# Two fp32 mixture-of-experts stages behind an attention: where w_out's parts, the weight sums and the routing are made

## The chip, the core and the metric

The kernel runs on one core of a Trainium2 chip. The core has five engines with instruction queues of their own: TensorE (PE; matmuls, whose weight loads are listed apart as PEld), VectorE (DVE), ScalarE (ACT), GpSimd (POOL) and SyncE (SP), which here only issues DMA transfers. The metric is the device time of one execution in microseconds; runs are given by their median.

## The reference

Three stages, each on the output of the one before, all in fp32:

```python
# 1. linear attention with decay, 4 x 8 heads, 768 steps, head size 64
state = gamma * state + k_t (outer) v_t;   y_t = scale * q_t @ state
# 2. x is 3072 x 512; w_a, w_b are 512 x 1536, w_out is 1536 x 512
x = ((x @ w_a) * (x @ w_b)) @ w_out
# 3. eight experts, one per token: w1 is 512 x 1024, w2 is 1024 x 512
e = argmax(x @ w_gate)
out = softmax(x @ w_gate)[e] * sigmoid(x @ w_output_gate)[e] * (relu(x @ w1[e]) @ w2[e])
```

## The kernel before

**Precision.** An fp32 operand is split into a high and a low part (a rounded copy and the difference), and `mm3` (L107 to L110) makes one product of three matmuls: high by high, high by low, low by high. "Parts" below always means this pair.

**Token groups.** The second stage runs over 3072 tokens in four groups. Tokens 0 to 511 and 512 to 1023 are the direct groups j = 0 and j = 1: for each of 12 tiles f of 128 hidden units `proj` makes both projections, `gate` their product with its split (`gs`, L576 and L579), and `down` adds the tile before to four token tiles. Tokens 1024 to 2047 and 2048 to 3071 are j = 2 and j = 3. For these `block_of_sums` (L706) makes each hidden tile for 1024 tokens from seven products of quarter matrices (quarters of x and of the weights, their sums and differences: B11, B21, B22 and U1 to U4; the weight side of a tile lies in two *units*, loaded from the DRAM tensor `q_d` by `load_unit`), 6 matmuls of 512 columns each on the two banks p0 and p1. The results are combined on VectorE (a1 at L721, g2 at L735, b2 at L738, a1 at L746), GpSimd multiplies one half (L739) and VectorE the other, which is split (`gs`, L748 and L749). `down` adds the first 512 tokens at once; the second 512 wait in `later` for `later_pass` (L760), which splits them tile by tile (`later_split`, L754 to L757) and makes their down product.

**w_out.** `wo_d` in DRAM holds w_out in fp32. For each tile of each pass after the first (j = 1, both blocks, both later passes; 60 in all) `load_wo` (L537) loads 256 KB two tiles ahead and `split_wo` makes the parts, the high one on ScalarE (L545), the low one by a subtraction on GpSimd (L546; two on VectorE).

**Weight sums.** During j = 1 `sum_steps` loads for each of 12 tiles 512 KB, makes four sums and differences on GpSimd (L626), splits them on ScalarE and VectorE (L630, L631), and stores 1 MB to `q_d`. `x_steps` makes the sums and splits of x's quarters for a block (L660, L666), three of them on GpSimd.

**Attention** runs beside the second stage, in 12 chunks of 256 steps (4 to 7 in j = 1, 8 to 11 in the first block), in batches: decay products `qd` (L149) and `vd` (L158) on VectorE, or on GpSimd for the chunks in `Q_POOL` and `V_POOL`, then scores and outputs on TensorE.

**Routing.** Each of 24 tiles of 128 tokens gets its expert and its place in the table `tab_d`. On TensorE (`on_pe`) that is a transpose (L301), the logits (L310) and a rank matmul (L340). On VectorE (`on_dve`) a tile is loaded again (`x2r`, L359), eight dot products with the gate's columns `wcol` follow (`s_d`, L365), then the argmax (`s_m`, L370), upon which GpSimd gathers for each token the column of its expert's output gate (`wx`, an indirect transfer, L374), then the dot product with it (`s_o`, L396 to L402), and the rank (`s_r`, L344 to L349). Tiles 2 to 7 are routed so in the first block, 8 to 15 in the second, 0 and 1 on TensorE in j = 1.

**What sets the order.** Each engine works in program order, and the order is written out by hand: `slot()` is called at fixed places (3 in each tile of a direct group, 7 in each tile of a block, 1 in a later pass), and `spread` deals lists of steps over a range of slots. An instruction that waits holds up everything behind it on its engine; a DMA that waits on SyncE holds up the queue.

```python
def mm3(outp, wh, wl, rh, rl, start, stop, more=False):
    pe.matmul(outp, lhsT=wh, rhs=rh, start=start, stop=False, skip_group_check=more)
    pe.matmul(outp, lhsT=wh, rhs=rl, start=False, stop=False, skip_group_check=more)
    pe.matmul(outp, lhsT=wl, rhs=rh, start=False, stop=stop, skip_group_check=more)
```

## Time and profile before

| | us |
|---|---|
| three runs | 1086.79, 1082.97, 1084.02 (median 1084.02) |
| the profiled execution | 1076.0 |
| its span, first to last instruction | 1074.3 |
| TensorE busy | 995.1 (93%), 7314 matmuls |
| VectorE, ScalarE, GpSimd busy | 633.0, 398.7, 318.2 |
| mean granted clock of TensorE | 0.977 |

The stretches of the program, by TensorE's instructions in the trace: the start to 27 us, j = 0 to 142, j = 1 to 292, the first block to 470, its later pass to 515, the second block to about 680, its later pass to 741, then the experts to the end. A row of the profile that names a wait gives what the engine waited for; where it stands in the program follows from the tile's name and the line.

### The profile page before, as it was taken

Reading aid. Unit: us, or ns where it says so; the run is one execution under the profiler, and the core shown is the slowest. Engines: PE = TensorE matmul, PEld = TensorE weight load, DVE = VectorE, ACT = ScalarE, POOL = GpSimd, SP = SyncE. Lnnn points to the kernel's source line nnn. Section 1 sums busy time; section 2 is a strip of 40 time slices with the busy share of each in tenths; the row PEclk is TensorE's granted clock in tenths of the full one; section 3 lists DMA queues with packets and bytes.
Section 4 is the critical chain, followed back from the end, with each engine's and each line's share of the span. In section 5 each row is a group of like instructions: output and inputs, shape, how many; then the busy total and the mean of one; then the engine's idle time right before and its main releaser. Section 6 shows DMA issues by size and latency. Waiting matters only on the chain. (4 is left out here: it accounts for less than half of the span.)

```text
span 1074.3 us, 19807 instructions
## 1 busy us (share of the span) xinstructions
PE 995.1 (93%) x7314; PEld 802.6 (75%) x7315; DVE 633.0 (59%) x1383; ACT 398.7 (37%) x768; POOL 318.2 (30%) x282
## 2 busy tenths in 40 slices
PE   6899999869899999989899999788699999999997
PEld 5688887757667777767677777567589988889886
DVE  5899955644846666648466666466255553445541
ACT  3676742323422222235222222245154443344431
POOL 3211014856511222237232323242222220203211
PEclk8999999989899999999899999899999999999999
DMA  6999965989786564533655654333166553536620
GB/s 245 341 327 300 297 207 196 303 325 372 261 310 225 191 227 161 161 117 88 226 173 191 170 206 133 130 129 105 23 196 195 186 160 116 169 97 194 204 87 28
DMA packets 72776, 208.70 MB, mean 194 GB/s; under 512 B 12717, under 2 KB 22189, under 8 KB 67888
## 3 DMA queue, kind: packets, MB, share of 16 engines
q1 hardware_dynamic: 65520, 187.95, 53.5%
q0 software_dynamic: 6544, 18.41, 5.0%
q8 instruction: 82, 1.34, 0.5%
q10 hardware_dynamic: 576, 0.56, 0.1%
q14 instruction: 54, 0.44, 0.1%
HBM read 162.79 MB, written 45.01 MB: 193 GB/s over the span
## 5 line engine op out<-in xcount | busy, mean ns | idle before, releaser
L546 POOL TENSOR_TENSOR wos<-wo,wos 128x512 fp32r<-128x512 f32 x58 | 84.2, 1452 | 95.1 <-ACT wos L545 39.6
L888 DVE TENSOR_TENSOR ew<-wraw,ew 128x512 fp32r<-128x512 f32 x112 | 77.1, 690 | 55.0 <-ACT ew L887 54.5
L108 PE MATMUL ph<-xe,ew 128*128 128x384 f32 (+4 forms) x288 | 98.2, 341 | 1.8 <-DVE x L599 1.1
L854 DVE SCALAR_TENSOR_TENSOR hs<-ph,hs 128x384 fp32r<-128x384 f32 (+4 forms) x72 | 39.1, 543 | 97.0 <-ACT hs L853 97.0
L109 PE MATMUL ph<-xe,ew 128*128 128x384 f32 (+4 forms) x288 | 95.2, 331 | 0.3 <-DVE xe L839 0.3
L110 PE MATMUL ph<-xe,ew 128*128 128x384 f32 (+4 forms) x288 | 95.3, 331 | 0.0
L874 POOL DMA_INDIRECT out<-y,idx x27 | 27.2, 1006 | 228.3 <-ACT y L873 214.6
L887 ACT CAST ew<-wraw 128x512 fp32r<-128x512 f32 x112 | 68.9, 616 | 55.7 <-PE acc L110 51.6
L108 PE MATMUL p<-U,unit 128*128 128x512 f32 x192 | 77.8, 405 | 10.1 <-DVE b L738 8.3
L108 PE MATMUL acc<-ew,hs 128*128 128x512 f32 (+1 forms) x216 | 85.7, 397 | 1.2 <-DVE hs L854 1.2
L108 PE MATMUL acc<-wos,gs 128*128 128x512 f32 x192 | 81.3, 424 | 4.7 <-ACT gs L576 3.8
L109 PE MATMUL acc<-ew,hs 128*128 128x512 f32 (+1 forms) x216 | 85.4, 396 | 0.0
L110 PE MATMUL acc<-ew,hs 128*128 128x512 f32 (+1 forms) x216 | 85.0, 394 | 0.0
L108 PE MATMUL p<-xs,ar 128*128 128x512 f32 x192 | 78.7, 410 | 5.2 <-DVE g_sb L571 2.8
L365 DVE SCALAR_TENSOR_TENSOR junkd<-x2r,wcol 128x512 bf16<-128x512 f32 x112 | 76.7, 685 | 10.3 <-DMA x2r<-x_d 9.4
L110 PE MATMUL acc<-wos,gs 128*128 128x512 f32 x192 | 78.5, 409 | 2.3 <-DVE gs L749 1.6
L853 ACT ACTIVATE hs<-ph 128x384 fp32r<-128x384 f32 (+4 forms) x72 | 34.5, 479 | 118.7 <-PE ph L110 112.4
L109 PE MATMUL acc<-wos,gs 128*128 128x512 f32 x192 | 77.1, 402 | 0.0
L110 PE MATMUL p<-xs,ar 128*128 128x512 f32 x192 | 75.8, 395 | 0.3
L110 PE MATMUL p<-U,unit 128*128 128x512 f32 x192 | 75.7, 394 | 0.0
L109 PE MATMUL p<-xs,ar 128*128 128x512 f32 x192 | 75.5, 393 | 0.0
L109 PE MATMUL p<-U,unit 128*128 128x512 f32 x192 | 75.5, 393 | 0.0
(207 smaller groups left out, 2308.0 us busy)
## 6 DMA issues: line engine op xcount, KB each, us to landing
wraw<-in_ex SPq DMA_DIRECT2D x64, 512.0 KB, 3.9
unit<-q_d SPq DMA_DIRECT2D x24, 1024.0 KB, 5.5
unit<-q_d SPq DMA_DIRECT2D x24, 768.0 KB, 4.5
wo<-wo_d SPq DMA_DIRECT2D x60, 256.0 KB, 3.9
wide<-in_w_ab SPq DMA_DIRECT2D x24, 512.0 KB, 6.0
q_d<-qsum SPq DMA_DIRECT2D x12, 1024.0 KB, 7.5
qk<-in_qk SPq DMA_DIRECT2D x23, 512.0 KB, 6.6
vk<-in_vk SPq DMA_DIRECT2D x23, 512.0 KB, 7.4
```

Of the source, the lines that this page charges most:

```text
L108: pe.matmul(outp, lhsT=wh, rhs=rh, start=start, stop=False, skip_group_check=more)
L109: pe.matmul(outp, lhsT=wh, rhs=rl, start=False, stop=False, skip_group_check=more)
L110: pe.matmul(outp, lhsT=wl, rhs=rh, start=False, stop=stop, skip_group_check=more)
L365: dve.scalar_tensor_tensor(junk, st["x2"], 1.0, wcol[e], op0=ALU.mult, op1=ALU.mult, accum_out=st["lg"][:, e : e + 1])
L546: (eng or pool).tensor_tensor(w[:, 1], t, f32(w[:, 0]), op=ALU.subtract)
L853: act.activation(h[:, 0, :n], p[:, :n], AF.Relu)
L854: dve.scalar_tensor_tensor(h[:, 1, :n], p[:, :n], 0.0, f32(h[:, 0, :n]), op0=ALU.max, op1=ALU.subtract)
L874: st = pool.indirect_dma_start(out=out[:, :], out_offset=bass.IndirectOffsetOnAxis(ap=ix[:, 1:2], axis=0), in_=y, in_offset=None, bounds_c ...
L887: act.copy(ew[f][:, part, 0], t[:, part])
L888: dve.tensor_tensor(ew[f][:, part, 1], t[:, part], f32(ew[f][:, part, 0]), op=ALU.subtract)
```

## The change

- **w_out's parts in DRAM.** In j = 1 the parts of each tile are made as before (the load now goes into the place of the low part) and stored to a new DRAM tensor `wos_d`, 512 KB a tile. The blocks and later passes load both parts from there (`next_wos`, three buffers); 48 loads of 256 KB, 48 copies and 48 subtractions are gone.
- **Weight sums.** `sum_steps` is gone from j = 1. In the first block GpSimd makes the sums of tile f + 1 during tile f, ScalarE and VectorE write their parts straight into the two units (`make_unit`), and these are stored for the second block (`store_unit`). What a unit holds of the seven quarters is regrouped (`UNIT_Q`).
- **Sums of x**, and two splits of an expert's weights, go from GpSimd to VectorE. Decay products `qd` of chunks 4 to 7 go to VectorE, those of chunks 8 to 11, and their `vd`, to GpSimd.
- **Routing.** Tiles 0 and 1 on VectorE in j = 1, tiles 2 to 7 on TensorE in the first block, tiles 8 to 15 on VectorE in the second block, now in two groups of four: the dot products go column by column over the four tiles, the gate's columns being loaded in pairs, and then come the tiles' argmaxes, gated dot products and ranks.
- **Smaller moves.** The first split of a later pass stands ahead of the block's last product; the first expert's table read and gathers, which stood at the end of the second block, stand in the first slot of the later pass.

```diff
-ON_DVE = range(2, 16)
+ON_DVE = [0, 1, *range(8, 16)]
...
-Q_POOL, V_POOL = {1, 2, 3, 4, 5, 6, 7}, {1, 2, 3}
+Q_POOL, V_POOL = {1, 2, 3, 8, 9, 10, 11}, {1, 2, 3, 8, 9, 10, 11}
...
-        def s_d(e):
...
+        def s_d(col, e):
             junk = lp(1).tile([128, 512], BF16, tag="junkd", name="junkd")
-            dve.scalar_tensor_tensor(junk, st["x2"], 1.0, wcol[e], op0=ALU.mult, op1=ALU.mult, accum_out=st["lg"][:, e : e + 1])
+            dve.scalar_tensor_tensor(junk, st["x2"], 1.0, col[:, e % 2], op0=ALU.mult, op1=ALU.mult, accum_out=st["lg"][:, e : e + 1])
...
     def on_dve(tiles):
 
         rs = [route_steps(i) for i in tiles]
-        out, ends = [rs[0][0], lambda: None], []
-        for r, n in zip(rs, rs[1:] + [None]):
-            for e, step in enumerate(r[1:9]):
-                out.append(step)
-                if ends and e in (2, 5):
-                    out.append(ends.pop(0))
-                if n and e == 4:
-                    out.append(n[0])
-            out.append(r[9])
-            ends = r[10:]
-        return out + [lambda: None] + ends
+        cols = []
+
+        def s_w():
+            e0 = 2 * len(cols)
+            if e0 < E:
+                cols.append(lp(2).tile([128, 2, 512], F32, tag="wraw", name="wcol"))
+                sync.dma_start(cols[-1].rearrange("p e n -> p (e n)"), bass.AP(a["wgt"].tensor, a["wgt"].offset + e0 * DM, [[0, 128], [1, 2 * DM]]))
+
+        out = [lambda: (s_w(), *[r[0]() for r in rs]), s_w, lambda: None]
+        for e in range(E):
+            for r in rs:
+                out.append(lambda r=r, e=e: r[1](cols[e // 2], e))
+            if e % 2:
+                out.append(s_w)
+        out += [rs[0][2], lambda: None]
+        for t, r in enumerate(rs):
+            if t + 1 < len(rs):
+                out += [r[3], rs[t + 1][2], r[4]]
+            else:
+                out += [r[3], r[4]]
+        return out
...
-    passes = [(j, f) for j in (1, 2, "2d", 3, "3d") for f in range(NF1)]
-
-    def load_wo(j, f, ahead=0):
-        n = passes.index((j, f)) + ahead
-        if n < len(passes):
-            t = p2.tile([128, 512], F32, tag="wo", name="wo")
-            sync.dma_start(t, wo_d[passes[n][1]])
-            rawq["wo", *passes[n]] = t
-
-    def split_wo(j, f, ahead=0, eng=None):
-        n = passes.index((j, f)) + ahead
-        if n < len(passes):
-            t = rawq.pop(("wo", *passes[n]))
-            w = p2.tile([128, 2, 512], F32R, tag="wos", name="wos")
-            act.copy(w[:, 0], t)
-            (eng or pool).tensor_tensor(w[:, 1], t, f32(w[:, 0]), op=ALU.subtract)
-            wos[passes[n]] = w
+    def load_wo(f):
+        if f < NF1:
+            w = wos[1, f] = lp(3).tile([128, 2, 512], F32R, tag="wos", name="wos")
+            sync.dma_start(f32(w[:, 1]), wo_d[f])
+
+    def split_wo(f):
+        if f < NF1:
+            w = wos[1, f]
+            act.copy(w[:, 0], f32(w[:, 1]))
+            pool.tensor_tensor(w[:, 1], f32(w[:, 1]), f32(w[:, 0]), op=ALU.subtract)
+
+    passes = [(j, f) for j in (2, "2d", 3, "3d") for f in range(NF1)]
+
+    def next_wos():
+        if passes:
+            key = passes.pop(0)
+            w = wos[key] = lp(3).tile([128, 2, 512], F32R, tag="wos", name="wos")
+            sync.dma_start(f32(w), wos_d[key[1]])
...
-    def sum_steps():
-        w, t = {}, {}
-
-        def s_load(f):
-            w[f] = room(2 * (f % 2), [128, 8, 256], F32, "wsum")
-            sync.dma_start(w[f][:, :4].rearrange("p (a q) n -> p a (q n)", a=2), wab_d[f])
-
-        def s_add(f):
+        sync.dma_start(q_d[f][:, 4], f32(ar[f][:, 1, :, 256:]))
+
...
+    def load_weights(f):
+        if f < NF1:
+            w = raw_w[f] = room(10, [128, 8, 256], F32, "wsum")
+            sync.dma_start(w[:, :4].rearrange("p (a q) n -> p a (q n)", a=2), wab_d[f])
+
+    def sum_weights(f):
+        if f < NF1:
+            w = raw_w[f]
             for out, x, y, op in ((5, 2, 3, ALU.add), (4, 5, 0, ALU.subtract), (6, 0, 2, ALU.subtract), (7, 1, 4, ALU.subtract)):
-                pool.tensor_tensor(w[f][:, out], w[f][:, x], w[f][:, y], op=op)
-
-        def s_split(f):
...
-        steps = [lambda: s_load(0), lambda: (s_load(1), s_add(0)), lambda: s_split(0)]
-        for f in range(NF1):
-            if f + 1 < NF1:
-                steps.append(lambda f=f: s_add(f + 1))
-            steps.append(lambda f=f: (s_store(f), f + 2 < NF1 and s_load(f + 2)))
...
+                pool.tensor_tensor(w[:, out], w[:, x], w[:, y], op=op)
+
+    def make_unit(n):
+
+        if n < 2 * NF1:
+            f, h = divmod(n, 2)
+            t = new_unit(2, n)
+            k = 1 if h else 2
+            q0 = UNIT_Q[h][0]
+            sync.dma_start(f32(t[:, :k]), q_d[f][:, q0 : q0 + k])
+            w = raw_w[f][:, 6:8] if h else raw_w[f][:, 4:6]
+            act.copy(t[:, k : k + 2, 0], w)
+            return lambda: dve.tensor_tensor(t[:, k : k + 2, 1], w, f32(t[:, k : k + 2, 0]), op=ALU.subtract)
+        return lambda: None
+
+    def store_unit(n):
+        if n < 2 * NF1:
+            f, h = divmod(n, 2)
+            k = 1 if h else 2
+            q0 = UNIT_Q[h][0] + k
+            sync.dma_start(q_d[f][:, q0 : q0 + 2], f32(units[2, n][:, k : k + 2]))
...
-            less(pool, "U3", "B22", "B12"),
+            less(dve, "U3", "B22", "B12"),
             split(dve, "U1"),
             less(dve, "U2", "B22", "U1"),
             split(dve, "U2"),
-            split(pool, "U3"),
+            split(dve, "U3"),
             less(dve, "U4", "B21", "U2"),
-            split(pool, "B22"),
+            split(dve, "B22"),
...
     def block_of_sums(j, slot):
+        fresh = j == 2
         for f in range(NF1):
-            load_wo(j, f, 2)
+            next_wos()
...
             product(r, u, 1, "B21", True)
             a1 = p1.tile([128, 512], F32, tag="a_sb", name="a1")
             act.copy(a1, r)
+            if fresh:
+                sum_weights(f + 1)
             slot()
             if f:
                 down(j, f - 1, [0])
             product(q, u, 0, "B11", True)
             dve.tensor_tensor(a1, a1, q, op=ALU.add)
+            if fresh and f:
+                store_unit(2 * f + 1)
             slot()
...
             product(q, u, 2, "U2", False)
             act.copy(g2, q)
-            load_unit(j, 2 * f + 3)
+            if fresh:
+                low0 = make_unit(2 * f + 2)
+            else:
+                load_unit(j, 2 * f + 3)
             slot()
             u = units.pop((j, 2 * f + 1))
-            product(r, u, 1, "B22", False)
+            product(r, u, 2, "B22", False)
             dve.tensor_tensor(g2, g2, r, op=ALU.add)
+            if fresh:
+                low0()
+                low1 = make_unit(2 * f + 3)
             slot()
-            product(q, u, 0, "U3", False)
+            product(q, u, 1, "U3", False)
             dve.tensor_tensor(b2, b2, q, op=ALU.add)
             pool.tensor_tensor(g2, g2, b2, op=ALU.mult)
+            if fresh:
+                low1()
+                load_weights(f + 2)
             slot()
             if f:
                 down(j, f - 1, [2, 3])
                 wos.pop((j, f - 1))
-            split_wo(j, f, 1)
-            product(q, u, 2, "U4", False)
+            if f == NF1 - 1:
+                next_wos()
+                gd0 = later_split(0)
+            product(q, u, 0, "U4", False)
             dve.tensor_tensor(a1, a1, q, op=ALU.mult)
             gs = p2.tile([128, 2, 512], F32R, tag="gs", name="gs")
             act.copy(gs[:, 0], a1)
             dve.tensor_tensor(gs[:, 1], a1, f32(gs[:, 0]), op=ALU.subtract)
             gt[j, f] = gs
-            load_unit(j, 2 * f + 4)
+            if fresh:
+                store_unit(2 * f + 2)
+            else:
+                load_unit(j, 2 * f + 4)
             slot()
+        return gd0
...
-        gd = later_split(0)
...
-            load_wo(key, f, 2)
+            if 0 < f < NF1 - 1:
+                next_wos()
...
             for i, tag in enumerate(("p1", "p0", "acc0", "acc1")):
                 if f == 0 and i == 2:
                     between()
+                    next_wos()
                 if i == 2 and f + 1 < NF1:
                     nxt = later_split(f + 1)
...
-            split_wo(key, f, 1, eng(f))
...
-                lines += [(on_pe([0, 1]), 4, 16), (sum_steps(), 9, 30), (x_first, 27, 31), (x_rest, 30, 36)]
+                lines += [(on_dve([0, 1]), 4, 28), (x_first, 27, 31), (x_rest, 30, 36)]
...
-        load_cols()
-        slot, flush = spread([(attention_steps(3), 0, 78), (on_dve(range(2, 8)), 6, 82)])
-        block_of_sums(2, slot)
+                load_wo(0)
+
+        sync.dma_start(wos_d[NF1 - 1], f32(wos[1, NF1 - 1]))
+        store_unit(0)
+        store_unit(1)
+        slot, flush = spread([(attention_steps(3), 0, 78), (on_pe(range(2, 8)), 6, 82)])
+        gd = block_of_sums(2, slot)
...
-        first = lambda: (load_idx0(0), gather(0, 0, T - TAIL), gather(0, 1, T - TAIL))
-        slot, flush = spread([([], 0, 1), ([*on_dve(range(8, 16)), fill_gap, first], 2, 82)])
-        block_of_sums(3, slot)
+        slot, flush = spread([([], 0, 1), ([*on_dve(range(8, 12)), *on_dve(range(12, 16))], 2, 82)])
+        gd = block_of_sums(3, slot)
...
         def load_expert(f):
-            split_raw(("ex", 0, f), f, pool if f in (1, 3) else dve)
+            split_raw(("ex", 0, f), f, dve)
             if f + 2 < NF2:
                 load_raw(("ex", 0, f + 2), a["ex"][0, f + 2])
 
         loads = [lambda f=f: load_expert(f) for f in range(6)]
+        first = lambda: (load_idx0(0), gather(0, 0, T - TAIL), gather(0, 1, T - TAIL))
         route = on_pe(range(16, 20))
...
-        slot, flush = spread([(loads, 0, 12), (turns, 0, 2), (route, 2, 12)])
-        later_pass(3, slot, lambda: between(3, 2048), lambda f: dve if f % 4 == 3 else pool)
+        slot, flush = spread([(loads, 0, 12), ([fill_gap, first], 0, 1), (route, 1, 11), (turns, 6, 10)])
+        later_pass(3, gd, slot, lambda: between(3, 2048))
```

VectorE in the second block, around one tile's argmax (MAX), the operation on the gathered column (`wx`) and the block's own operations on p0 and p1 (`a`, `b`, `later`, `gs`), before:

```order
L370 MAX mx<-lg 128x8
L372 MAX_INDEX ix<-mx,lg 128x8
L382 CAST ixf<-ix 128x1
L384 TENSOR_SCALAR oh<-iota_113,ixf 128x8
L387 TENSOR_SCALAR nm<-mx 128x1
L738 TENSOR_TENSOR b_6313<-b_6313,p_6283 128x512
L365 SCALAR_TENSOR_TENSOR junkd,lg<-x2r,wcol 128x512
L746 TENSOR_TENSOR a_6290<-a_6290,p_6283 128x512
L749 TENSOR_TENSOR gs<-a_6290,gs 128x512
L365 SCALAR_TENSOR_TENSOR junkd,lg<-x2r,wcol 128x512 x2
L396 SCALAR_TENSOR_TENSOR junkd,og<-x2r,wx 128x512
```

and the same place of the changed kernel, from the second of four tiles' argmax to the end of its `wx` steps:

```order
L372 MAX mx<-lg 128x8
L374 MAX_INDEX ix<-mx,lg 128x8
L384 CAST ixf<-ix 128x1
L386 TENSOR_SCALAR oh<-iota_117,ixf 128x8
L389 TENSOR_SCALAR nm<-mx 128x1
L346 TENSOR_TENSOR ohsum<-ohsum,oh 128x8
L349 SCALAR_TENSOR_TENSOR junk_6171,sf<-rp,oh 128x8
L351 CAST si<-sf 128x1
L398 SCALAR_TENSOR_TENSOR junkd,og<-x2r,wx 128x512
L402 TENSOR_SCALAR eo<-eo 128x1
L403 SCALAR_TENSOR_TENSOR den<-sm,eo 128x1
L404 RECIPROCAL pay<-den 128x1
```

Three dot products (L365) and three operations of the block stood between MAX and `wx`; now only a rank (`ohsum`, `sf`, `si`) stands there, of the tile before, and for the other tiles that or one or two operations of the block.

GpSimd in the second half of j = 1, with the weight sums (`wsum`), w_out's subtraction (`wos`) and the decay products (`qd`), before:

```order
L626 TENSOR_TENSOR wsum<-wsum 128x256 x4
L546 TENSOR_TENSOR wos<-wo,wos 128x512
L149 TENSOR_TENSOR qd<-qk,dec 128x512
L626 TENSOR_TENSOR wsum<-wsum 128x256 x4
L223 TENSOR_TENSOR kept<-state,gc 128x128
L626 TENSOR_TENSOR wsum<-wsum 128x256 x4
L546 TENSOR_TENSOR wos<-wo,wos 128x512
L149 TENSOR_TENSOR qd<-qk,dec 128x512
L626 TENSOR_TENSOR wsum<-wsum 128x256 x4
L546 TENSOR_TENSOR wos<-wo,wos 128x512
```

and after, from the routing's gathers to the first two tiles' sums:

```order
L376 DMA wx<-in_wog,ix 128x512
L541 TENSOR_TENSOR wos<-wos 128x512
L376 DMA wx<-in_wog,ix 128x512
L352 DMA tab_d<-pay,si 24576x4
L225 TENSOR_TENSOR kept<-state,gc 128x128
L541 TENSOR_TENSOR wos<-wos 128x512
L352 DMA tab_d<-pay,si 24576x4
L151 TENSOR_TENSOR qd<-qk,dec 128x512
L160 TENSOR_TENSOR vd<-vk,vtab 128x512
L541 TENSOR_TENSOR wos<-wos 128x512 x2
L642 TENSOR_TENSOR wsum<-wsum 128x256 x8
```

The sums of all but the first two tiles have left the stretch, and the decay products here are those of the next chunks, for the first block.

SyncE in the second later pass, with w_out's loads (`wo`, `wos`), the expert's weights (`wraw`) and the stores of x (`x_d`), before:

```order
L451 DMA wraw<-in_ex 128x1024 x2
L537 DMA wo<-wo_d 128x512
L605 DMA x_d<-x_7122 128x512
L605 DMA x_d<-x_7125 128x512
L605 DMA x_d<-x_7128 128x512
L605 DMA x_d<-x_7131 128x512
L451 DMA wraw<-in_ex 128x1024
L537 DMA wo<-wo_d 128x512 x2
L451 DMA wraw<-in_ex 128x1024
L537 DMA wo<-wo_d 128x512 x2
L451 DMA wraw<-in_ex 128x1024
L537 DMA wo<-wo_d 128x512 x2
```

and after:

```order
L452 DMA wraw<-in_ex 128x1024 x2
L607 DMA x_d<-x_7021 128x512
L607 DMA x_d<-x_7024 128x512
L607 DMA x_d<-x_7027 128x512
L607 DMA x_d<-x_7030 128x512
L549 DMA wos<-wos_d 128x1024
L452 DMA wraw<-in_ex 128x1024
L836 DMA idx<-tab_d 128x2x4
L549 DMA wos<-wos_d 128x1024 x2
L452 DMA wraw<-in_ex 128x1024
L549 DMA wos<-wos_d 128x1024 x2
L452 DMA wraw<-in_ex 128x1024
```

A load of both parts stands where the fp32 load stood, and an index read of the first expert stands among them.

## Rows read from the trace of the kernel before

**Rows 1.** Busy us by stretch and engine (instructions); TensorE's clock, DMA share, GB/s.

```profile
142.00:292.00 150.00, 130.41 (x1484) 102.53 (x1483) 83.42 (x146) 46.83 (x82) 81.48 (x80) 0.94 0.85 292
292.00:470.00 178.00, 173.06 (x1609) 132.17 (x1608) 113.13 (x316) 45.30 (x98) 45.16 (x37) 1.00 0.61 203
515.00:680.00 165.00, 156.07 (x655) 119.40 (x654) 100.33 (x309) 39.45 (x84) 47.64 (x38) 0.98 0.55 178
```

**Rows 2.** Waits of TensorE, 142 to 292: releaser, us, times, longest.

```profile
PE sc L209 <- POOL qd L149: 8.5, 2, 7.7
PE acc L108 <- ACT gs L576: 3.8, 1, 3.8
```

**Rows 3.** Waits of TensorE: 470 to 515, 680 to 741, whole span.

```profile
PE p L109 <- POOL wos L546: 3.9, 4, 1.0
...
PE p L109 <- POOL wos L546: 7.2, 7, 2.4
...
PE p L108 <- ACT gd L756: 3.9, 2, 1.9
```

**Rows 4.** Waits of TensorE, 515 to 680.

```profile
PE p L108 <- DVE b L738: 5.2, 2, 4.4
```

**Rows 5.** Busy time of three short stretches.

```profile
472.00:476.00 4.00, 3.76 (x9) 2.74 (x10) 0.99 (x2) 0.19 (x1) 0.00 (x0) 0.57 0.24 64
286.00:292.00 6.00, 5.14 (x12) 3.69 (x13) 5.18 (x2) 1.71 (x3) 4.25 (x2) 0.54 0.54 213
568.00:572.00 4.00, 3.59 (x16) 2.96 (x17) 3.40 (x11) 0.88 (x2) 1.05 (x1) 1.00 0.47 190
```

**Rows 6.** Timeline: start, duration, engine, line, operation, [idle before, releaser].

```profile
230.57 2.88 POOL L626 TENSOR_TENSOR wsum<-wsum 128x256 f32<-128x256 f32 x4 [6.92 <-DMA wsum<-wab_d]
...
234.63 2.28 POOL L149 TENSOR_TENSOR qd<-qk,dec 128x512 f32<-128x512 f32 x1
...
236.96 0.54 PE L209 MATMUL sc<-qd,qk 64*64 64x64 f32 x6 [7.66 <-POOL qd L149]
```

**Rows 7.** Timeline of VectorE: a split in the same stretch.

```profile
277.26 1.73 DVE L579 TENSOR_TENSOR gs<-g_sb,gs 128x512 fp32r<-128x512 f32 x1 [0.69 <-ACT gs L576]
```

**Rows 8.** Timeline of TensorE: the routing of one tile between two matmuls.

```profile
713.62 0.39 PE L110 MATMUL acc<-wos,gd 128*128 128x512 f32 x1
713.85 0.60 PE L301 MATMUL pt<-ident,x 128*128 128x128 f32 x4
...
715.10 0.48 PE L108 MATMUL p<-wos,gd 128*128 128x512 f32 x1
```

**Rows 9.** Timeline of VectorE and GpSimd around one gather in the second block.

```profile
614.76 0.17 DVE L370 MAX8 mx<-lg 128x8 f32<-128x8 f32 x1
...
615.48 1.00 POOL L374 DMA_INDIRECT wx<-in_wog,ix  x1 [2.11 <-DVE ixf L382]
...
621.12 0.69 DVE L396 SCALAR_TENSOR_TENSOR junkd<-x2r,wx 128x512 bf16<-128x512 f32 x1 [2.18 <-DMA wx<-in_wog,ix]
...
622.55 0.67 DVE L735 TENSOR_TENSOR later<-later,p 128x512 f32<-128x512 f32 x1
```

**Rows 10.** Timeline of two more gathers; landing of all transfers into wx.

```profile
560.59 1.01 POOL L374 DMA_INDIRECT wx<-in_wog,ix  x1 [1.62 <-DVE ixf L382]
...
566.94 0.69 DVE L396 SCALAR_TENSOR_TENSOR junkd<-x2r,wx 128x512 bf16<-128x512 f32 x1 [2.90 <-DMA wx<-in_wog,ix]
...
669.60 1.02 POOL L374 DMA_INDIRECT wx<-in_wog,ix  x1 [2.62 <-DVE nm L387]
...
673.01 0.69 DVE L396 SCALAR_TENSOR_TENSOR junkd<-x2r,wx 128x512 bf16<-128x512 f32 x1 [2.53 <-DMA wx<-in_wog,ix]
...
DMA to landing us min/median/max: 3.1/5.3/6.9
```

**Rows 11.** DMA issues: count, KB each, median us to landing.

```profile
wraw<-in_ex SPq DMA_DIRECT2D x64, 512.0 KB, 3.9
...
wsum<-wab_d SPq DMA_DIRECT2D x12, 512.0 KB, 7.7
```

More of the change, by code (lines that the diff above doesn't have):

```diff
@@ L69, in lp @@
             early.close()
-            for k in (1, 2, 6):
+            for k in (1, 2, 3, 6):
                 late[k] = ctx.enter_context(tc.tile_pool(name=f"l{k}", bufs=k))
@@ L78, in attention_moe_moe2 @@
     wo_d = dram.tile([NF1, 128, DM], F32, name="wo_d")
+    wos_d = dram.tile([NF1, 128, 2, 512], F32, name="wos_d")
     wab_d = dram.tile([NF1, 128, 2, 512], F32, name="wab_d")
@@ L143, in prep_q @@
         if n in (2, 3):
-            both = p2.tile([128, 2, 512], F32, tag="wos", name="prep")
+            both = e2.tile([128, 2, 512], F32, tag="wos", name="prep")
             qd = both[:, 0].rearrange("p (u n) -> p u n", u=2)
@@ L406, in route_steps @@
         if i in ON_DVE:
[L407 removed]
+            return [s_x, s_d, s_m, s_o, s_r]
         return [s_t, s_l, s_r]
[L410 to L419 removed]
     def on_dve(tiles):
         rs = [route_steps(i) for i in tiles]
[L424 to L434 removed]
+        cols = []
[17 more added lines that the diff above has]
+        return out
     def on_pe(tiles):
@@ L511, in n_high @@
                 sync.dma_start(wo_d[key[1]], w)
-                ws = p2.tile([128, 2, 512], F32R, tag="wos", name="wos")
+                ws = e2.tile([128, 2, 512], F32R, tag="wos", name="wos")
                 wos[0, key[1]] = ws
@@ new lines, in keep_quarters, with new_unit, load_unit @@
+        sync.dma_start(q_d[f][:, 4], f32(ar[f][:, 1, :, 256:]))
+    units = {}
+    UNIT_AT = [7, XH, XL]
+    UNIT_Q = [(0, 4), (4, 7)]
+    raw_w = {}
+    def new_unit(j, n):
+        t = units[j, n] = room(UNIT_AT[n % 3], [128, 3 if n % 2 else 4, 2, 256], F32R, "unit")
+        return t
+    def load_unit(j, n):
+        if n < 2 * NF1:
+            q0, q1 = UNIT_Q[n % 2]
+            sync.dma_start(f32(new_unit(j, n)), q_d[n // 2][:, q0:q1])
+    def load_weights(f):
+        if f < NF1:
+            w = raw_w[f] = room(10, [128, 8, 256], F32, "wsum")
+            sync.dma_start(w[:, :4].rearrange("p (a q) n -> p a (q n)", a=2), wab_d[f])
@@ L682, in x_steps @@
         return first, rest
-    units = {}
-    UNIT_AT = [7, XH, XL]
-    def load_unit(j, n):
-        if n < 2 * NF1:
-            f, h = divmod(n, 2)
-            t = units[j, n] = room(UNIT_AT[n % 3], [128, 3 if h else 4, 2, 256], F32R, "unit")
-            sync.dma_start(f32(t), q_d[f][:, 4:] if h else q_d[f][:, :4])
     def product(out, u, q, x, start):
@@ L1061, in attention_moe_moe2 @@
         spare.clear()
-        tri_f = p2.tile([128, 2, 128], F32, tag="wo", name="tri_f")
+        tri_f = p1.tile([128, 2, 128], F32, tag="tri_f", name="tri_f")
         def constants():
@@ L1112, in attention_moe_moe2 @@
                 ta = act_a(pa, n)
+                if j:
+                    split_wo(f)
+                    if f == NF1 - 1:
+                        sum_weights(0)
                 slot()
@@ L1117, in attention_moe_moe2 @@
                 gate(j, f, ta, pb, n, 3 * f + 1 if f and j == 0 else None)
-                if j and f == 9:
-                    load_unit(2, 0)
+                if j and f == NF1 - 2:
+                    load_weights(0)
+                if j and f == NF1 - 1:
+                    make_unit(0)()
                 slot()
@@ L1135, in attention_moe_moe2 @@
                         dve.tensor_copy(ohsum, base8)
-                else:
-                    split_wo(1, f, 1)
                 if f == NF1 - 1:
+                    if j:
+                        next_wos()
                     down(j, f, tiles)
@@ L1158, in between @@
             evac_x2(tok0, range(4), (1, 3))
-        later_pass(2, slot, lambda: between(2, 1024))
+        later_pass(2, gd, slot, lambda: between(2, 1024))
         flush()
```

39 lines of the change are left out of this document (11 added, 28 removed).

## The prediction

> **What bounds the kernel now.** I read the profile in the order in which it narrows. First the busy time by stretch of the program [rows 1]: TensorE is busy for 130.4 of 150 us in the second direct group (142 to 292), 173.1 of 178 in the first block of sums (292 to 470) and 156.1 of 165 in the second (515 to 680). TensorE bounds everything, so an edit gains only what TensorE stands still in its own stretch (19.6, 4.9 and 8.9 us), what its clock loses there, and the work that it is spared or given. Then the waits of TensorE by stretch: in the direct group the largest is a decay product of GpSimd, 8.5 us, then a split for 3.8 [rows 2]; in the two later passes it waits for w_out's parts, 3.9 and 7.2 us, and for the first split, 3.9 in both together [rows 3]; in the second block half of the idle time is one wait of 4.4 [rows 4]. A wait costs more than its length: in the stretch 472 to 476, behind the 1.9 us for the first split, the granted clock is 0.57, and 286 to 292, behind the 3.8, has 0.54, while 568 to 572, which holds a shorter wait, has 1.00 [rows 5]. Such a stretch of 4 us loses about 4 x 0.43 = 1.7 us, one of 6 about 2.8. The profiled execution took 1076.0 us, 8.0 below the median of the runs, 1084.02; I sum against the 1076.0 and apply the difference to the median.
>
> **Second direct group: -23.** The longest wait is read from one place [rows 6]: GpSimd starts four weight sums at 230.57 (2.88 us), then w_out's subtraction, then the decay product at 234.63 (2.28 us), and TensorE, which needs that product, starts at 236.96 after 7.66 us. The change takes 12 sets of four sums (12 x 2.9 = 35 us) off GpSimd in this stretch, and the sums of x as well, and gives the decay products of these chunks to VectorE, where an operation of 128x512 takes 0.67 (622.55 in [rows 9]). It also takes 12 loads of 512 KB and 12 stores of 1 MB from the queue and adds 12 stores of 512 KB. The other waits are of the same kind: GpSimd late, or a VectorE operation stretched beside it (the split at 277.26 took 1.73 us [rows 7]). Gone: 19.6 us of waits, about 2.7 of lost clock, and the routing of two tiles on TensorE, which lasts from 713.85 to 715.10 for one tile [rows 8], 1.25 us, with switching about 1.3. That is 24.9. VectorE takes over two tiles' dot products and two gathers; it is busy for 83 of 150 us now and stays near 80, since the splits of the sums leave it. I leave 2 us for what comes late next: -23. Bounds: -25 if all goes, -16 if half of the waits other than the 7.66, and their clock, return. The cover for these edits is VectorE's idle time; without it each of them would cost its own duration, 0.7 us.
>
> The sums are not gone, they run in the first block. There the row of 277.26 bears on them: if each of the 44 sums, of some 0.7 us, held up VectorE for its length, that would be 31 us, and VectorE has 178 - 113 = 65 us free there [rows 1], so I add nothing beyond the waits below. In the Trainium skill, "SBUF — State Buffer", section "SBUF: two separate sides", VectorE with two SBUF inputs and GpSimd reading SBUF hold one shared port pair in turn, each for a whole instruction; by that rule the sums would stretch VectorE there as the row shows, and the sum stays the same.
>
> **First block: +7.5.** Six tiles go to TensorE: 6 x 1.3 = 7.8 us. VectorE is spared 48 dot products and six gathers, so I take the old 4.9 us of waits as gone. New: the first units wait for the first sums (1.5, about one product), and GpSimd makes the sums one tile ahead. A tile lasts 178/12 = 14.8 us; the load took 7.7 in a busy stretch [rows 11] and the sums take 2.9, so they fit. But a unit needs load, sums, copy and split in turn, and the decay products of chunks 8 to 11 stand behind the sums on GpSimd: 3 us in all, a guess between nothing and one wait of 7.66. 7.8 - 4.9 + 1.5 + 3 = 7.4. Bounds: +4 with none, +16 if each tile's unit comes 0.7 to 1 us late.
>
> **Later passes: -5 and -6.** A load takes the place of a load, a copy and a subtraction for each tile. In the first pass the wait for the split (1.9), its clock (1.7) and 3.9 for w_out go: 7.5. The first split now stands ahead of the last product, and in its place comes the split of the block's last tile, 0.7; the third tile's load stands behind four stores of x on SyncE's queue and is late by up to its landing (loads of this size: 3.9 [rows 11]); I take 1.8. After that loads run two tiles ahead, 24 matmuls of 0.23 (713.62 to 713.85 [rows 8]), 5.5 us, more than 3.9. So -5 (bounds -7, 0). In the second pass 1.9, 7.2 and 2.5 of clock go, 11.6; new are 0.7 and 2 likewise, and 3 because loads of w_out stand on the queue behind loads of an expert's weights that wait for VectorE. So -6 (bounds -10, 0).
>
> **Second block: +22, the largest single risk.** Eight tiles are routed on VectorE, in two groups of four, and the order decides. Before, three dot products and two or three operations of the block stand between a tile's argmax and the operation that needs the gathered column. After, there stand one operation of the block or only a rank. Before, an argmax starts at 614.76, its gather on GpSimd at 615.48, and VectorE waits 2.18 and starts at 621.12, although it had three dot products in between; the block's next operation follows at 622.55 [rows 9]. So a gather takes L = 5.64 there, from its start on GpSimd to VectorE's; in two other places where VectorE waited it took 3.41 and 6.35, and the landings of all 14 lie between 3.1 and 6.9, median 5.3 [rows 10].
>
> After the change each tile costs VectorE 0.71 (614.76 to 615.48) + L + 1.43 (621.12 to 622.55), in which it does next to nothing else, four times in a row. With an operation of the block ahead (0.69), the last one of a product with the split of the hidden tile (2.1) and one sum (0.67) between the tiles, that is 0.69 + 4 x (0.71 + L + 1.43) + 2.77 = 12.0 + 4L. TensorE's work from the same place to the same place, one hidden tile and two more products with half a down product, is 16.4 us (72 matmuls of 0.2285). What VectorE is late by is covered up to some 1.4: its wait of 2.18 gave TensorE one of 0.8 (5.2 - 4.4 [rows 4]). So a group costs TensorE 12.0 + 4L - 16.4 - 1.4 = 4L - 5.8. Transfers compete less while TensorE stands, which speaks for a short L, the median for a long one; I take the middle of 3.4 and 5.3, L = 4.35: 11.6 us for a group, 23.2 for two. The clock falls once in each (2 x 1.75 = 3.5), and the old waits go, all but the first, which is for loads of x that stay where they are: 8.9 - 4.4 = 4.5. 23.2 + 3.5 - 4.5 = 22.2. In short 8L - 12.6. Bounds: L = 3.4 gives +14.6, L = 6.3 gives +37.8; hidden gathers would give about 0.
>
> After 741 nothing of weight changes.
>
> **Sum.** -23 + 7.5 - 5 + 22 - 6 = -4.5: 1071.5 of 1076.0, and 1079.5 of 1084.02.
>
> **Rivals.** (1) *The gathers are quick.* At the shortest seen, L = 3.4, the second block costs 14.6 and the sum is -12: 1072; hidden gathers would give -26.5: 1057.5. For it: while VectorE and TensorE stand, few transfers are under way. Against it: the median. In the Trainium skill, "DMA: Bandwidth & Descriptors", section "Anatomy of one DMA — SWDGE (gpsimd) path", a transfer issued by GpSimd takes about 2.0 us plus its bytes at 436 GB/s; for these 256 KB that is 2.6 us, an estimate, and by it the sum would be near -18, 1066. The trace's median of 5.3 disagrees, its shortest of 3.1 is nearer. (2) *The gathers are as slow as the slowest*, because 512 KB of w_out per tile now run beside the units' 1.75 MB instead of 256 KB: L = 6.3, second block +37.8, sum +11: **1095.5, slower**. Its place is VectorE's wait for wx, eight times; it turns the whole change to a loss from L = 4.9 on. (3) *The loads of w_out are not hidden in the later passes*: 512 KB in 2.74 us is 191 GB/s, with the expert's weights beside it. The 11 us gained there don't come: 1090.5. Against it: the stretches of [rows 1] moved 178 to 292 on average. (4) *The sums come late in the first block*, up to 1 us for each tile: +16 there, 1088.
>
> **How the numbers follow.** Forecast (L 3.8 to 5.0, 1075 to 1085): 0.38. Quick gathers (1057 to 1075): 0.25. Slow gathers (1085 to 1096): 0.2. Loads not hidden: 0.1. Late sums: 0.07. The predicted time is the first one's, 1079.5. The range of 1065 to 1096 leaves out the far half of the quick gathers and a little at the other end. A measurement of this kernel can tell about 0.3% (3.3 us) from no change: below 1080.8 lie a good half of the forecast and the quick gathers, 0.47; from 1080.8 to 1087.3 most of the rest of the forecast and some of the slow and late cases, 0.23; above, 0.30.
>
> **What would show it.** In the second direct group the waits for GpSimd's decay product are gone and the stretch is near 127 us; the first block is near 185, with six tiles' transposes and logits on TensorE; the second is near 187, with eight waits of VectorE for wx, the largest new wait in the profile, and the granted clock down in two places; the later passes are near 40 and 54 with no wait for w_out's subtraction. The forecast is wrong if VectorE's waits for wx are short or TensorE doesn't feel them, if TensorE waits in the first block for units, or if the later passes wait for the loaded parts.

## The result, and the profile after

The changed kernel takes 1067.53 us (median of four runs, 1065.97 to 1069.11), the kernel before beside it 1083.72: a ratio of 0.9845, 95% interval 0.9820 to 0.9871. The forecast was 1079.5, in a range of 1065 to 1096; so the sign was right and the gain, 16.2 us, three to four times the forecast's 4.5.

The two profiled executions differ by less: 1076.0 and 1068.46 us. By stretch of the program (from first matmul to first matmul; the wait for the first split counts to its later pass):

| stretch | before | after | difference | forecast |
|---|---|---|---|---|
| second direct group | 150.3 | 126.0 | -24.3 | -23 |
| first block | 178.2 | 191.1 | +12.9 | +7.5 |
| its later pass | 45.0 | 38.2 | -6.8 | -5 |
| second block | 165.2 | 177.6 | +12.4 | +22 |
| its later pass | 60.4 | 46.5 | -13.9 | -6 |
| experts, to the end | 333.4 | 345.5 | +12.1 | 0 |

The six differ by -7.6, and without the experts by -19.7. Two later profiles of the kernel before give 163.5 and 164.2 us for the second block, so that row is good to about 2 us. Busy time by stretch of the changed kernel, columns as in [rows 1]:

```profile
141.80:267.80 126.00, 123.17 (x1462) 98.48 (x1461) 74.50 (x175) 33.71 (x67) 33.22 (x30) 0.97 0.78 257
267.80:458.90 191.10, 182.19 (x1682) 142.95 (x1681) 93.41 (x232) 54.66 (x121) 74.19 (x76) 0.98 0.64 220
458.90:497.10 38.20, 36.16 (x157) 29.02 (x156) 23.98 (x27) 16.24 (x23) 0.00 (x0) 1.00 0.69 235
497.10:674.70 177.60, 159.08 (x653) 120.18 (x652) 102.63 (x308) 32.70 (x73) 33.89 (x28) 0.97 0.60 206
674.70:721.20 46.50, 43.88 (x226) 35.18 (x225) 26.21 (x86) 20.38 (x44) 6.71 (x6) 1.00 0.71 233
```

The direct group stands still for 2.8 us instead of 19.6, and GpSimd is busy there for 33 us instead of 81. The later passes run at a granted clock of 1.00, the upper level. The first block stands for 8.9, the second for 18.5. TensorE's waits over the whole span (of [rows 2] and [rows 3] the decay product in this group, w_out's subtraction and the first split are gone):

```profile
PE p L110 <- DVE b L761: 15.2, 8, 5.8
PE acc L110 <- ACT gs L776: 8.4, 5, 3.7
...
PE acc L110 <- ACT hs L885: 4.7, 3, 2.7
PE p L110 <- DMA wos<-wos_d: 4.4, 4, 1.9
```

The first two are the two blocks, the third the experts, the fourth the waits for the loads of w_out's parts in the later passes. A gather in the second block, which answers to [rows 9] (timeline of VectorE, GpSimd and TensorE):

```profile
570.60 0.16 DVE L372 MAX8 mx<-lg 128x8 f32<-128x8 f32 x1
...
571.31 0.99 POOL L376 DMA_INDIRECT wx<-in_wog,ix  x1 [5.18 <-DVE ixf L384]
...
574.82 0.69 DVE L398 SCALAR_TENSOR_TENSOR junkd<-x2r,wx 128x512 bf16<-128x512 f32 x1 [2.91 <-DMA wx<-in_wog,ix]
...
576.25 0.67 DVE L736 TENSOR_TENSOR a<-a,p 128x512 f32<-128x512 f32 x1
```

0.71 from the argmax to the gather and 1.43 behind it, as forecast; but L is 3.51, not the 5.64 of [rows 9]. The eight are 3.40, 3.51, 3.32, 3.37, 3.31, 4.28, 3.38 and 3.35; VectorE waits for seven of them; during the eighth it waits for TensorE. The first block's largest wait (VectorE, ScalarE, TensorE):

```profile
277.77 1.25 DVE L654 TENSOR_TENSOR unit<-wsum,unit 128x512 fp32r<-128x512 f32 x1
...
282.80 0.62 ACT L653 CAST unit<-wsum 128x512 fp32r<-128x512 f32 x1 [5.06 <-DMA q_d<-unit]
...
283.99 0.75 DVE L252 TENSOR_TENSOR xraw<-xraw,y 128x256 f32<-128x256 f32 x2 [4.98 <-ACT xraw L247]
284.66 0.68 DVE L761 TENSOR_TENSOR b<-b,p 128x512 f32<-128x512 f32 x1
...
285.26 0.68 DVE L654 TENSOR_TENSOR unit<-wsum,unit 128x512 fp32r<-128x512 f32 x1
...
285.40 0.79 PE L110 MATMUL p<-U,unit 128*128 128x512 f32 x1 [5.84 <-DVE b L761]
```

ScalarE, about to write the fourth unit, stands for 5.06 us on the store of the first one, whose buffer it takes; a copy behind it on ScalarE keeps VectorE waiting, and TensorE waits for a bank that VectorE has yet to read.

### The profile page after: what moved, and what is told of

It is laid out like the page before. It is cut to its first block, busy times and chain, and to the rows that moved or that the text cites. A ratio compares the mean times of both kernels' runs of the same rounds, so it can differ in the third digit from the quotient of the medians.

```text
span 1066.7 us, 19808 instructions
## 1 busy us (share of the span) xinstructions
PE 995.8 (93%) x7362; PEld 808.5 (76%) x7363; DVE 584.9 (55%) x1329; ACT 373.9 (35%) x740; POOL 235.1 (22%) x232
## 5 line engine op out<-in xcount | busy, mean ns | idle before, releaser
L110 PE MATMUL p<-U,unit 128*128 128x512 f32 x192 | 79.0, 411 | 17.0 <-DVE b L761 15.2
L110 PE MATMUL acc<-wos,gs 128*128 128x512 f32 x192 | 79.0, 412 | 8.9 <-ACT gs L776 8.4
L762 POOL TENSOR_TENSOR later<-later,b 128x512 f32<-128x512 f32 x24 | 38.1, 1589 | 193.8 <-DVE b L761 193.7
L112 PE MATMUL acc<-wos,gs 128*128 128x512 f32 x192 | 77.2, 402 | 0.0
L112 PE MATMUL p<-U,unit 128*128 128x512 f32 x192 | 76.2, 397 | 0.0
L111 PE MATMUL p<-U,unit 128*128 128x512 f32 x192 | 76.2, 397 | 0.0
L111 PE MATMUL acc<-wos,gs 128*128 128x512 f32 x192 | 75.2, 392 | 0.0
L367 DVE SCALAR_TENSOR_TENSOR junkd<-x2r,wcol 128x512 bf16<-128x512 f32 x80 | 58.0, 725 | 8.8 <-DMA x2r<-x_d 7.5
```

What stands on the lines that cost most here:

```text
L367: dve.scalar_tensor_tensor(junk, st["x2"], 1.0, col[:, e % 2], op0=ALU.mult, op1=ALU.mult, accum_out=st["lg"][:, e : e + 1])
L762: pool.tensor_tensor(g2, g2, b2, op=ALU.mult)
```

## The experiments

**What emptied the direct group.** Three kernels start from the kernel before, which took 1074.7 us beside them.

The decay products alone:

```diff
-Q_POOL, V_POOL = {1, 2, 3, 4, 5, 6, 7}, {1, 2, 3}
+Q_POOL, V_POOL = {1, 2, 3}, {1, 2, 3}
```

> The kernel before with one part of the change: the decay products qd of chunks 4 to 7 go from GpSimd to VectorE. Theory that these products wait behind the weight sums on GpSimd: the 8.5 us of waits for them go, and with the clock behind them the time falls by 8 to 11 us (about 0.99 of before). Rival, that VectorE gets busy beside GpSimd and other waits take their place: -3 to +2 us.

1073.28 against 1074.72, a ratio of 0.9992 (0.9981 to 1.0003): the rival. The wait for `qd` on GpSimd is gone, and TensorE waits 5.1 us at another place for the same kind of product; the group takes 149.1 us where the kernel before, profiled beside it, takes 150.7 (timeline of GpSimd, ScalarE, VectorE and TensorE):

```profile
244.64 2.91 POOL L626 TENSOR_TENSOR wsum<-wsum 128x256 f32<-128x256 f32 x4 [4.97 <-DMA wsum<-wab_d]
...
247.59 1.04 ACT L630 CAST qsum<-wsum 128x1024 fp32r<-128x1024 f32 x1 [7.34 <-POOL wsum L626]
...
248.66 1.23 DVE L631 TENSOR_TENSOR qsum<-wsum,qsum 128x1024 fp32r<-128x1024 f32 x1 [7.68 <-ACT qsum L630]
...
250.47 0.68 DVE L149 TENSOR_TENSOR qd<-qk,dec 128x512 f32<-128x512 f32 x1
...
251.25 0.44 PE L209 MATMUL sc<-qd,qk 64*64 64x64 f32 x5 [5.08 <-issue]
```

GpSimd's sums wait for their load, ScalarE for the sums, VectorE for ScalarE, and `qd` at 250.47 stands behind all that on VectorE, 0.10 us before TensorE goes on. So here the product was late behind the chain of the sums on either engine. That chain begins with a load: the sums wait 4.97 us for it, and 6.92 in [rows 6], longer than four sums take (2.9).

The sums left out, with their loads, copies and stores kept (the kernel's later x is not the reference's, so the experts get other token counts; its 1299.88 us say nothing here, and only the stretch is read):

```diff
             for out, x, y, op in ((5, 2, 3, ALU.add), ...
-                pool.tensor_tensor(w[f][:, out], w[f][:, x], w[f][:, y], op=op)
+                pass
...
-            act.copy(t[f][:, :, 0], w[f][:, 4:])
+            act.copy(t[f][:, :, 0], w[f][:, :4])
...
```

> The kernel before without the 48 sums and differences of weights on GpSimd; the splits and stores then take the unsummed weights, so loads, copies and stores stay. Theory that GpSimd's 35 us of sums make most of the direct group's 19.6 us of waits: the group falls by 15 to 20 us, and the time with it (0.982 to 0.986). Rival, that the transfers (6 MB loaded, 12 MB stored there) or the sums of x make them: -8 us or less.

The group takes 138.8 us instead of 150.7, -11.9: less than the 15 to 20 of the theory, more than the rival's 8. TensorE's waits there:

```profile
PE acc L108 <- ACT gs L576: 3.8, 1, 3.8
...
PE sc L209 <- POOL qd L149: 1.2, 1, 1.2
PE acc L110 <- DVE gs L579: 0.7, 1, 0.7
```

The wait for `qd` falls from 8.0 to 1.2. The edit takes away both the sums and GpSimd's wait for their load, and can't tell the two apart. What is left at the end, 3.8 and 0.7 for the split of the last hidden tile, stands beside the sums of x, some of them on GpSimd, and is gone in the changed kernel, where VectorE makes all of them. So of the 24.3 some 12 are shown to be the weight sums. For the rest there is only a reckoning, as no run moves these parts alone: 4.5 with the fallen clock behind them (2.8 by [rows 5]) for the sums of x, 2.6 for the routing of two tiles, and 2.5 unassigned.

**The later passes.** The early first split alone, in the kernel before:

```diff
+            if f == NF1 - 1:
+                gd0 = later_split(0)
             product(q, u, 2, "U4", False)
...
-        gd = later_split(0)
```

> The kernel before with one part of the change: the first split of each later pass stands ahead of the last product of the block. Theory: the two waits of 1.9 us and the half clock behind them go, -5 to -7 us (0.994). Rival, that the wait for w_out's subtraction, or the split of the last hidden tile, takes their place: within 2 us of before.

1072.42 against 1074.72, 0.9985 (0.9972 to 0.9998): less than the theory's 5 to 7, and a little more than the rival's 2. The first pass with its block gains 3.1 us on the kernel before, profiled beside it, the second 0.6: there the waits for w_out's subtraction grow from 7.2 [rows 3] to 9.7.

```profile
PE p L109 <- POOL wos L546: 9.7, 7, 4.8
```

The loaded parts undone, in the changed kernel, in the later passes only:

```diff
+            if key[0] in ("2d", "3d"):
+                sync.dma_start(f32(w[:, 1]), wo_d[key[1]])
+            else:
                 sync.dma_start(f32(w), wos_d[key[1]])
...
             wos.pop((key, f))
+            split_late((key, f + 1))
```

> The changed kernel with one part undone: in the two later passes w_out is loaded in fp32 again (256 KB, as far ahead as now) and split on ScalarE and GpSimd one tile ahead; the early first split stays. Theory that the loaded parts gave most of the 20.8 us by which the two later passes became shorter: +9 to +14 us, with waits for w_out's subtraction like the 11 us before. Rival, that the early first split and the undisturbed clock gave them: +4 us or less.

1071.08 where the kernel before took 1074.15. The later passes take 39.7 and 63.0 us, against 38.2 and 46.5 of the changed kernel: 18.0 of the 20.7 us that it gained there come back, nearly all of it in the second, with this wait in it:

```profile
PE p L111 <- POOL wos L558: 13.8, 7, 5.2
```

This is more than the theory's 14: besides the waits, TensorE's busy time in the second pass is 4.8 us longer, with a granted clock of 0.92 over the pass (1.00 in the changed kernel). The comparison is of profiles alone, since the changed kernel wasn't run beside this one.

**The second block.** The changed kernel once more, and the argmaxes ahead:

> The changed kernel, unchanged. The four pauses of TensorE between the experts, 9.5 us in its first profile, were in neither profile of the kernel before. Theory: they belong to the changed kernel's program; then they are here again, and the gain on this chip is near 7.5 us (0.993), the rest of the 16 us of the first comparison being that chip's. Rival: they come and go with the chip or the execution; then they are absent here and the gain is 16 to 17 us (0.984).

1066.13 us where the kernel before took 1083.90, 0.9853 (0.9801 to 0.9905). Neither forecast holds whole: the pauses are there again, and the gain is 17.8 us all the same.

```diff
             for t, r in enumerate(rs):
                 out.append(lambda r=r, e=e: r[1](cols[e // 2], e))
+                if e == E - 1 and t < 2:
+                    out.append(r[2])
...
-        out += [rs[0][2], lambda: None]
         for t, r in enumerate(rs):
-            if t + 1 < len(rs):
-                out += [r[3], rs[t + 1][2], r[4]]
-            else:
-                out += [r[3], r[4]]
+            out += [r[3], r[4]]
+            if t + 2 < len(rs):
+                out.append(rs[t + 2][2])
```

> The changed kernel with another order in each group of four tiles: the first two argmaxes stand right behind their last dot product, and each later argmax one tile ahead, so that a rank, an argmax and a gated dot product of other tiles stand between a gather and its use (two gathers in flight). Theory that VectorE's waits for wx, 19.7 us in seven, are what costs the second block its 12 us: the waits fall below 8 us, the block from 177.6 to 166 to 170 us, the time by 8 to 12 us. Rival, that what delays TensorE is VectorE's own work in these stretches (eight argmaxes, ranks, gated products): the waits fall and the block stays within 3 us.

1054.73 beside the 1066.13, so -11.4, which is the middle of a wide spread: two of the four runs took 1049 us and two 1060 to 1061, and the profile is of a short one. All four lie below those of the changed kernel, and in the profiles the block takes 166.2 us instead of 178.0. VectorE's waits in the block, first the changed kernel's for wx, then this one's:

```profile
DVE junkd L398 <- DMA wx<-in_wog,ix: 19.5, 7, 3.8
...
DVE junkd L367 <- DMA x2r<-x_d: 5.6, 2, 3.7
DVE junkd L398 <- DMA wx<-in_wog,ix: 4.6, 3, 1.9
```

19.5 us of waiting for wx have become 4.6, with the same instructions in another order. The theory: the 11.8 us that the block gets back are nearly all of the 12.4 that it had lost.

The load for the dot products, by empty steps ahead of them:

```diff
-([*on_dve(range(8, 12)), *on_dve(range(12, 16))], 2, 82)
+([*(four := on_dve(range(8, 12)))[:2], *[lambda: None] * 6, *four[2:], *on_dve(range(12, 16))], 2, 82)
```

> The changed kernel with six empty steps between the loads for the first four tiles of the second block and the first dot product. Theory: VectorE's wait of 4.1 us for x2r and TensorE's of 4.9 behind it go, with the half clock: -5 to -8 us. Rival, that the later steps, now closer together, give it back in the gathers: -2 to +3 us.

1067.05 beside 1066.13, the block 178.2 instead of 178.0: the rival. The first wait falls from 4.6 to 0.8 us, and others take its place (TensorE in the block, then VectorE):

```profile
PE p L110 <- DVE a L736: 5.2, 1, 5.2
PE p L110 <- DVE b L761: 5.0, 3, 2.3
...
PE p L110 <- ACT b L742: 2.9, 1, 2.9
...
586.93 0.69 DVE L398 SCALAR_TENSOR_TENSOR junkd<-x2r,wx 128x512 bf16<-128x512 f32 x1 [6.00 <-DMA wx<-in_wog,ix]
```

The longest stands behind one gather, the fourth tile's, which took 6.60 us instead of 3.47. With the steps closer, the loads of x for the next four tiles start 7 us earlier, just ahead of it, and the DMA share while it ran was 1.02.

**The first block.** The store of the first unit ahead of the stores of x:

```diff
                     make_unit(0)()
+                    store_unit(0)
...
-        store_unit(0)
         store_unit(1)
```

> The changed kernel with the store of the first unit issued right behind its parts, ahead of the last down products, and not behind four stores of x. Theory: TensorE's wait of 5.8 us in the first block (ScalarE stands on the buffer of that unit, VectorE behind it) goes with the half clock behind it: -6 to -9 us. Rival, that the next load of raw weights or the sums are late then too: -2 to +2 us.

1065.88 beside 1066.13: nothing. ScalarE no longer stands, and TensorE now waits at the next tile's first product, for the load of the third unit's quarters, which SyncE reaches only behind the stores of x, of w_out's parts and of a unit, and some loads:

```profile
285.93 0.79 PE L110 MATMUL p<-B,unit 128*128 128x512 f32 x1 [4.54 <-DMA unit<-q_d]
```

With that load issued ahead of them too, and the argmaxes ahead:

```diff
                         load_weights(1)
+                        load_part(2)
```

> The changed kernel with the argmaxes ahead, the store of the first unit early, and the load of the third unit's raw quarters issued before the stores of x. Theory: the wait of 5.6 us in the first block, which only moved to that load when the store alone went early (4.5 us), goes now, with the half clock behind it: 5 to 9 us below the kernel with the argmaxes ahead alone, 0.966 to 0.971 of before where before takes 1084. Rival: it moves once more, to the next unit or the sums: within 2 us of that kernel.

1036.47 where the kernel before took 1074.15, 0.9644 (0.9624 to 0.9664). The block takes 185.1 us instead of 191.0 in the kernel with the argmaxes ahead alone: the theory's 5 to 9, read from the profiles, since the two kernels weren't run beside each other. And with four empty steps more for each group of four tiles:

```diff
-s_w, lambda: None]
+s_w, *[lambda: None] * (5 if len(tiles) == 4 else 1)]
```

> The kernel above with four more empty steps between the loads for each group of four tiles and its first dot product in the second block. Theory that VectorE's waits for x2r (5.6 us in two) cost TensorE 4.5 us and the half clock, and that giving them back, as in the earlier try, came from gathers without slack: -4 to -7 us against the kernel above. Rival, that the steps behind get too close: -1 to +3 us.

1030.54 beside the 1036.47, the second block 161.5 instead of 166.8: the theory. Six empty steps for the first group alone gave nothing while nearly every gather was waited for, and four for each group give 5.9 us now that two are in flight; that the slack of the gathers is the reason is argued, since the steps differ too. This kernel is the fastest, 0.9616 of before (0.9590 to 0.9641). Its two blocks and the pass between:

```profile
262.20:447.50 185.30, 179.89 (x1682) 140.55 (x1681) 93.01 (x232) 54.83 (x121) 74.24 (x76) 1.00 0.67 227
447.50:485.40 37.90, 36.17 (x157) 29.00 (x156) 23.99 (x27) 16.25 (x23) 0.00 (x0) 1.00 0.69 241
485.40:646.90 161.50, 155.22 (x653) 118.18 (x652) 102.51 (x308) 32.80 (x73) 34.44 (x28) 0.99 0.65 225
```

**The experts.** The change reaches only what leads up to them (the first expert's gathers, two splits of its weights), and they take 12.1 us more. Matmul by matmul, 9.8 of these come after the wait for `xg` (7.2 us in both): 1.3 in a stretch behind it with a granted clock of 0.57 (1.00 at the same place before), and nearly all the rest at four places (TensorE, and ScalarE ahead of the third):

```profile
836.92 0.50 PE L110 MATMUL acc<-ew,hs 128*128 128x512 f32 x1 [1.22 <-issue]
...
920.73 0.50 PE L110 MATMUL acc<-ew,hs 128*128 128x512 f32 x1 [1.12 <-ACT hs L885]
...
965.08 0.49 ACT L885 ACTIVATE hs<-ph 128x384 fp32r<-128x384 f32 x1 [7.87 <-remote]
...
965.62 0.50 PE L110 MATMUL acc<-ew,hs 128*128 128x512 f32 x1 [2.73 <-ACT hs L885]
...
1001.72 0.44 PE L110 MATMUL acc<-ew,hs 128*64 128x512 f32 x1 [1.47 <-issue]
```

These four cost 8.3 us, with the slower matmuls right behind them. In each, ScalarE makes the second relu of an expert 6.5 to 8.4 us after the first, where the kernel before takes 1.8 to 2.4, and TensorE goes on some 0.5 us after its start; a fifth expert's is as late, and TensorE doesn't wait. Each relu stands behind a branch on the number of the expert's tokens.

> The kernel before, unchanged, profiled once more. Its first profiled execution took 1076.0 us with no pause of TensorE between the experts, its timed runs 1083 to 1087; the changed kernel's profile has four pauses there, 9.5 us in sum, and lies among its timed runs. Theory: such pauses come and go with the execution, whatever the kernel; then this execution is either near 1076 without them or near 1084 with some 8 us of them. Rival: they belong to the changed kernel; then this one has none at any time.

1075.53, with experts of 333.0 us and no such place.

> The kernel before, unchanged, profiled a third time, beside the changed kernels below. Its median was 1083.7 and 1083.9 us where the changed kernel took 1067.5 and 1066.1, but 1074.7 where the first group of experiments ran, and both of its profiles (1076.0, 1075.5) are of the short kind. Theory: where it takes 1084 its profile shows pauses between the experts like the changed kernel's, some 9 us, and the pauses come with the chip and not with the change. Rival: it takes 1084 with no such pauses, and the 9 us lie in its blocks. If it takes 1075 here, the kernels below tell: pauses in them beside a before without any belong to the changed program.

1078.4, with experts of 334.3 and none. But the changed kernels beside it (the split undone, the unit ahead, the dots late) take 334.0, 335.7 and 334.9 there: no pauses either. Where the kernel before took 1083.7 and 1083.9, the five profiles of changed kernels give 345.5, 345.6, 341.6, 343.1 and 347.4. So the pauses don't follow from the change: in its variants they are there where the kernel before takes 1084 and not where it takes 1075. Nor do they come with the chip alone, as an expectation had it: the record names the same one for a group of either kind (1074.7 and 1083.9). That they are also what makes it 1084 fits in size (9 us) but isn't shown, since no profile of the kernel before fell there. What delays those operations is open.

## Why the prediction was right, and where its sum was off

- **Second direct group: right** (-23, measured -24.3). Its reading of [rows 6] was right in that the sums on GpSimd are the cause of the largest wait, and wrong in two points. It took the 7.66 us for the time of the sums and what follows them, though GpSimd had waited 6.92 us for the sums' load just before. And the decay products' move to VectorE, which it counted in, gave nothing clear of the noise when made alone.
- **First block: short by 5.4.** The routing's 7.8 is there (TensorE is busy for 182.2 instead of 173.1 us, the fallen clock included). The failing term is the waits: 8.9 us in place of 4.9, where I had put 4.5. Two thirds are one wait that I hadn't seen: ScalarE on the buffer of a unit that is still being stored. The sums themselves kept up: in the block TensorE waited for no unit. They stretch VectorE as the row of 277.26 said: a split of a unit that began while GpSimd was at its sums (275.53 to 278.48), at 277.77, took 1.25 us, the next one, at 285.26, 0.68. That agrees with the rule of the Trainium skill ("SBUF — State Buffer", section "SBUF: two separate sides"), and no wait of TensorE is put down to it.
- **Later passes: -20.7 for -11.** Here two terms of the second pass were mis-sized. The new waits, put at 5.7, measured 2.5, three waits for a load; the fallen clock, put at 2.5, was worth up to 5.4 (TensorE is busy for 43.9 us instead of 49.3 with the same matmuls, at a granted clock of 1.00 instead of 0.94). Another 1.8 are small waits for the routing and the first expert's x, which the sum left out.
- **Second block: +12.4 for +22.** The mechanism was right: the gathers of the eight tiles, with seven waits for wx, VectorE's largest new one, which nearly go with another order. The failing term is L, taken as 4.35 and measured as 3.49 on average. With that 8L - 12.6 is +15.3. The rest is the cover: TensorE's waits in the two groups of tiles are 6.2 and 5.4 us, where 4L - 5.8 gives 8.2, so either more than 1.4 us of lateness is covered or TensorE had more work there than 16.4. It was rival 1, quick gathers, to which the prediction gave 0.25. Its reason fits: the DMA share while the seven waited gathers ran was 0.24 to 0.55, while the 5.64 of [rows 9] and the 6.35 of [rows 10] ran 0.74 and 0.69, and 0.24 while the 3.41 did. That the engines stand isn't enough: VectorE stood for 6.0 of the 6.60 us of the gather at a share of 1.02 above, and TensorE behind it. Nor does the share alone set the time: another gather of that run took 3.27 at 0.72. In the fastest kernel, where TensorE runs on, the gathers land in 3.6 to 6.0 us again, 4.7 in the median. By the page ("DMA: Bandwidth & Descriptors", section "Anatomy of one DMA — SWDGE (gpsimd) path", of the Trainium skill) the estimate was 2.6 us; no gather here took less than 3.0 from its start to its use.
- **Base.** The sum was made against a profile of 1076.0 whose kernel takes 1084 elsewhere. The five terms measure -19.7; in the medians, 16.2 and 17.8 us were gained. On the 1084.02 those -19.7 would give 1064.3, just below the stated range; with what the sum left out, the experts' 12.1 and the 8 us between the two bases, the measured time lies inside. That the range held is in part luck.

## What to carry to other kernels

An operation that is late behind a chain on one engine can be just as late behind the same chain on another: look for where the chain begins, and move the chain. A gather's wait is hidden well by a second one in flight. Freeing an earlier wait gives something only when the steps behind it have slack, and it can move other loads beside a gather. When a buffer's store holds up its next writer, look at all that stands ahead of store and load on the issuing queue: moving one of them alone here only moved the wait to the other.

## What wasn't expected of the hardware

The same kernel before took 1083.7 and 1083.9 us in two groups of runs and 1074.7 and 1074.2 in two others, and the changed kernels' experts lasted 342 to 347 us in the first kind and 334 to 336 in the second, with pauses of TensorE of up to 2.7 us at the second relu of an expert. A gather of 256 KB that VectorE waited for took 3.3 to 4.3 us from its start to its use in the changed kernel's second block, at a DMA share of 0.24 to 0.55 beside it, and 6.60 in one place at 1.02.
